# Second expert layer: second product by Strassen's scheme over pairs of weight blocks for two thirds of the tokens, with every prepared weight part kept in DRAM

## The chip, the cores and the metric

The kernel runs on one core of a Trainium2 chip. The metric is device time in microseconds (us): the median of three runs of the kernel before is 2180.21 us (2179.23 to 2182.91).

## What is computed

Three stages follow one another; all data are float32.

```python
# attention over pooled keys, 4 batches, 8 heads, 576 positions -> x [2304, 512]
x = (sigmoid(x @ w_gate) * (x @ w_val)) @ w_out        # first layer, inner width 1536
P = exp(x @ moe2_w_gate - max)                         # [2304, 8], then 8 rounds of row/column scaling
out = 0
for e in range(8):                                     # second layer, all 8 experts on all tokens
    h = maximum(x @ w1[e], 0.0)                        # w1[e]: 512 x 1024
    out += P[:, e:e+1] * (h @ w2[e])                   # w2[e]: 1024 x 512
```

Only the second layer changes. Every product is taken in three passes: each operand is split into a high part and a low part (value minus high), and high x high, high x low and low x high are summed.

## The kernel before

**Blocks and steps.** The 2304 tokens are 6 blocks of 384 (`TB`), taken as 3 pairs (`p`). For each pair the second layer walks 8 experts (`e`) and 4 quarters (`q`) of the inner width: 3 x 8 x 4 = 96 steps, the list `steps2` (L666). A step covers 256 inner columns (two halves of 128) for 768 tokens, and has two products.

**First product** (x with w1) goes by Strassen's scheme in Winograd's form: seven products P1 to P7 (L885) in place of eight, each 6 matmuls of 384 columns (`product`, L895). The sums of token blocks were stored earlier to DRAM (`xd`) and are loaded once per pair (`load_xf`, L722). The sums of w1 quarters are made in every step: `prep_w1` (L683) splits the raw weights into high parts (ScalarE) and low parts (GpSimd), tiles `fa` and `fs`. The results are combined in PSUM and in `c` tiles by VectorE, and `hidden` (L913) writes relu, high part (ScalarE) and low part (VectorE).

**Second product** (h with w2) is plain: `y_chunk` (L922) takes one chunk of 128 tokens: 6 matmuls of 512 columns into one PSUM bank `big`, and VectorE adds the bank, times the gate, to a running sum `acc`. A step has 6 chunks, which belong to the step before, so that they stand between P1 to P7 and give the other engines time. The weights are split in every step by `prep_w2` (L711).

**What sets the order.** The program is recorded in a hand-written order (`manual_schedule`); each engine runs its own instructions in that order and waits on semaphores. After each product a slot (`slot2`) issues one piece of weight preparation. All DMAs of this part are issued from SP's queue, in program order. `bank(tag, n)` hands out PSUM banks in rotation: 4 `big`, 2 `at`, 2 `gv`.

The weights of an expert's quarter are loaded and split three times, once per pair of token blocks.

Of the kernel before, what the change touches and what calls it, by code (L numbers as in the profile page):

```python
# [20 lines left out]
def attention_moe_moe_kernel(  # L21
# [647 lines left out]
    def load_w1(n):
        if n < len(steps2):  # L670
            _, e, q = steps2[n]
            raw1[n] = pools["late"].tile([128, 4, 2, 128], F32, tag="raw1", name="raw1", bufs=2)
            nc.sync.dma_start(out=raw1[n].rearrange("p a k f -> p (a k f)"), in_=moe2_w1[e, q])

    def load_w2(n):
        if n < len(steps2):
            _, e, q = steps2[n]
            raw2[n] = pools["more"].tile([128, 2, DM], F32, tag="raw2", name="raw2", bufs=2)
            nc.sync.dma_start(
                out=raw2[n], in_=moe2_w2[e].rearrange("(h g p) d -> g p h d", h=2, p=128)[q]  # L680
            )

    def prep_w1(n):  # L683


        if n >= len(steps2):
            return
        raw = raw1.pop(n)
        pool = pools["more" if n % 2 else "late"]
# [31 lines left out]

    def load_xf(p, i):  # L722
        if p < NPAIR:
            xf[p, i] = pools["late"].tile([128, 2, 2, TB], F32R, tag=f"xf{i}", name=f"xf{i}", bufs=1)
            nc.sync.dma_start(out=f32(xf[p, i]).rearrange("p s k c -> p (s k c)"), in_=xd[p][i])

    with tc.manual_schedule():
# [167 lines left out]
        def product(n, name, pt, start):  # L895

            (which, i), x = PRODUCTS[name]
            w = wsum[n][which]
            t = xf[steps2[n][0], x]
            m = 0  # L900
            for k in range(2):
                for s, o in PASSES:
                    nc.tensor.matmul(  # L903
                        out=pt[:, :TB],
                        lhsT=w[:, s, i, k],
                        rhs=t[:, o, k],
                        start=(start and m == 0),
                        stop=(m == 5),
                        skip_group_check=True,
                    )  # L910
                    m += 1
# [145 lines left out]
        for t in (3, 4, 5, 0, 1, 2):  # L1057
            y_chunk(len(steps2) - 1, t)
# [59 lines left out]
```

## Time and profile before

| | |
|---|---|
| median of 3 runs | 2180.21 us |
| span of the profiled execution | 2185.2 us |
| attention and first layer (to about 662 us) | the profile's first third |
| second layer, first pair of blocks (32 steps) | 684 to 1171 us, after a start-up from 662 us |
| second and third pair (64 steps) | 1170.9 to 2171.6 us |
| last chunks after the last step | 2171.6 to the end |
| TensorE busy over the span | 96% |

The profile shows one execution. "PE" is TensorE's matmuls, "PEld" its weight loads (one before each matmul), DVE is VectorE, ACT is ScalarE, POOL is GpSimd, SPq is SP's DMA queue. The time between the starts of two neighbouring matmuls is what a matmul costs in a stream; its own record is longer, since matmuls are pipelined.

### The profile page before, as it was taken

Reading aid. Unit: us, or ns where it says so; the run is one execution under the profiler, and the core shown is the slowest. Engines: PE = TensorE matmul, PEld = TensorE weight load, DVE = VectorE, ACT = ScalarE, POOL = GpSimd, SP = SyncE. Lnnn points to the kernel's source line nnn. Section 1 sums busy time; section 2 is a strip of 40 time slices with the busy share of each in tenths; the row PEclk is TensorE's granted clock in tenths of the full one; section 3 lists DMA queues with packets and bytes.
Section 4 is the critical chain, followed back from the end, with each engine's and each line's share of the span. In section 5 each row is a group of like instructions: output and inputs, shape, how many; then the busy total and the mean of one; then the engine's idle time right before and its main releaser. Section 6 shows DMA issues by size and latency. Waiting matters only on the chain.

```text
span 2185.2 us, 28656 instructions
## 1 busy us (share of the span) xinstructions
PE 2096.2 (96%) x10973; PEld 1905.0 (87%) x10973; DVE 1422.6 (65%) x2172; ACT 882.5 (40%) x1607; POOL 891.5 (41%) x780
## 2 busy tenths in 40 slices
PE   4679999999999999999999999999999999999999
PEld 4568989988997888888888898989888888898988
DVE  6846876644435877666666666666666666666665
ACT  4334343454544444434343434343433343434342
POOL 1100000353554465454545454545454545454541
PEclk8679999999999999999999999999999999999999
DMA  7432553453562132121215121212125212121211
GB/s 227 143 119 85 167 171 116 131 181 106 194 228 92 59 116 78 61 75 60 76 59 206 58 78 58 78 58 78 58 78 188 77 58 78 58 78 58 78 58 39
DMA packets 87451, 222.09 MB, mean 102 GB/s; under 512 B 8849, under 2 KB 8849, under 8 KB 87313
## 3 DMA queue, kind: packets, MB, share of 16 engines
q1 hardware_dynamic: 82128, 210.81, 28.5%
q10 hardware_dynamic: 5184, 9.44, 1.2%
q8 instruction: 86, 1.41, 0.3%
q14 instruction: 53, 0.43, 0.1%
HBM read 189.55 MB, written 30.67 MB: 101 GB/s over the span
## 4 chain that ended last, share of the span: by engine, by line
PE 86%; DVE 6%; issue 3%; ACT 2%; DMA 1%; POOL 1%; SPq 0%; ACTq 0%; DVEq 0%; POOLq 0%
PE big L934 37%; PE at L903 18%; PE gv L903 14%; PE gv L268 10%; PE big L560 4%; DVE wa_lo L236 1%; PE at L351 1%; DMA narrow<-made 1%; PE at L437 1%; DVE made L166 1%; DVE made L165 1%; DVE g L821 1%; ACT wa_hi L231 1%; PE at L422 0%; DVE wide L175 0%
## 5 line engine op out<-in xcount | busy, mean ns | idle before, releaser
L934 PE MATMUL big<-w2hl,h 128*128 128x512 f32 x3456 | 893.8, 394 | 0.0
L934 PEld LDWEIGHTS big<-w2hl,h 128*128 128x128 f32 x3456 | 642.0, 188 | 102.2
L963 DVE SCALAR_TENSOR_TENSOR acc<-big,prob,acc 128x512 f32<-128x512 f32 x516 | 385.6, 748 | 264.8 <-PE big L934 258.7
L705 POOL TENSOR_TENSOR fa<-raw,fa 128x768 fp32r<-128x768 f32 x96 | 179.4, 1869 | 440.0 <-PE big L934 403.2
L268 PE MATMUL gv<-xs,wa_hi 128*128 128x384 f32 x1152 | 314.6, 355 | 20.9 <-ACT xs L447 8.1
L707 POOL TENSOR_TENSOR fs<-ss,fs 128x512 fp32r<-128x512 f32 x96 | 125.0, 1303 | 292.9 <-ACT fs L704 289.3
L268 PEld LDWEIGHTS gv<-xs,wa_hi 128*128 128x128 f32 x1152 | 217.1, 198 | 28.2 <-ACT xs L447 8.9
L917 ACT ACTIVATE h<-gv 128x384 fp32r<-128x384 f32 x192 | 94.3, 491 | 355.2 <-DVE gv L1045 196.4
L903 PE MATMUL at<-xf,fa 128*128 128x384 f32 x1152 | 233.7, 338 | 0.8 <-DVE c L1038 0.8
L903 PE MATMUL at<-xf,fs 128*128 128x384 f32 x1152 | 232.4, 337 | 0.4 <-ACT c L1011 0.4
L903 PE MATMUL gv<-xf,fs 128*128 128x384 f32 x1152 | 231.6, 336 | 0.0
L717 DVE TENSOR_TENSOR w2hl<-raw,w2hl 128x512 fp32r<-128x512 f32 x192 | 227.6, 1186 | 6.1 <-ACT w2hl L716 6.1
L903 PEld LDWEIGHTS at<-xf,fa 128*128 128x128 f32 x1152 | 206.6, 189 | 17.7 <-DVE c L1038 1.6
L903 PEld LDWEIGHTS gv<-xf,fs 128*128 128x128 f32 x1152 | 205.4, 188 | 16.3
L268 PE MATMUL gv<-xs,wa_lo 128*128 128x384 f32 x576 | 203.1, 353 | 14.8 <-DVE wa_lo L236 11.8
L903 PEld LDWEIGHTS at<-xf,fs 128*128 128x128 f32 x1152 | 204.4, 188 | 9.0 <-ACT c L1011 0.7
L918 DVE SCALAR_TENSOR_TENSOR h<-gv,h 128x384 fp32r<-128x384 f32 x192 | 107.2, 558 | 107.6 <-ACT h L917 107.6
L560 PE MATMUL big<-h,wa_hi 128*128 128x384 f32 x576 | 150.8, 343 | 0.0
L594 POOL TENSOR_TENSOR fx<-x,fx 128x768 fp32r<-128x768 f32 x10 | 18.4, 1844 | 316.5 <-DVE x L577 263.4
L236 POOL TENSOR_TENSOR wa_lo<-stage,wa_hi 128x512 fp32r<-128x512 f32 x67 | 99.6, 1499 | 81.3 <-ACT wa_hi L231 69.6
L268 PEld LDWEIGHTS gv<-xs,wa_lo 128*128 128x128 f32 x576 | 114.7, 199 | 17.7 <-DVE wa_lo L236 14.6
L708 POOL TENSOR_TENSOR fs<-ss,fs 128x512 fp32r<-128x512 f32 x96 | 125.5, 1307 | 0.0
(149 smaller groups left out, 2682.1 us busy)
## 6 DMA issues: line engine op xcount, KB each, us to landing
raw<-in_moe_w_dram SPq DMA_DIRECT2D x192, 512.0 KB, 3.8
stage<-narrow SPq DMA_DIRECT2D x150, 256.0 KB, 2.8
xd<-fx SPq DMA_DIRECT2D x21, 768.0 KB, 3.3
xf<-xd SPq DMA_DIRECT2D x21, 768.0 KB, 6.6
narrow<-made ACTq DMA_DIRECT2D x36, 256.0 KB, 2.0
wide<-in_moe_w_gate_dram SPq DMA_DIRECT2D x12, 512.0 KB, 3.8
wide<-in_moe_w_val_dram SPq DMA_DIRECT2D x12, 512.0 KB, 10.0
wide<-in_moe_w_out_dram SPq DMA_DIRECT2D x12, 512.0 KB
```

What stands on the lines that cost most here:

```text
L236: eng.tensor_tensor(out=lo, in0=raw, in1=f32(hi), op=ALU.subtract)
L268: nc.tensor.matmul(out=out_, lhsT=a[s], rhs=b[m], start=(i == 0), stop=(i == n - 1))
L560: nc.tensor.matmul(out=x2p[d][:, :TB], lhsT=w[s][:, d * 128 : (d + 1) * 128], rhs=gs[j, f][m], start=(first and i == 0), stop=(last and i ...
L705: pl(out=fa[:, 1], in0=raw[:, 0:3], in1=f32(fa[:, 0]), op=ALU.subtract)
L707: pl(out=fs[:, 1, 0:2], in0=ss[:, 0:2], in1=f32(fs[:, 0, 0:2]), op=ALU.subtract)
L708: pl(out=fs[:, 1, 2:4], in0=ss[:, 2:4], in1=f32(fs[:, 0, 2:4]), op=ALU.subtract)
L717: nc.vector.tensor_sub(out=t[:, 1, i], in0=raw[:, i], in1=f32(t[:, 0, i]))
L903: nc.tensor.matmul(out=pt[:, :TB], lhsT=w[:, s, i, k], rhs=t[:, o, k], start=(start and m == 0), stop=(m == 5), skip_group_check=True,)
L917: nc.scalar.activation(out=t[:, 0], in_=src, func=AF.Relu)
L918: nc.vector.scalar_tensor_tensor(out=t[:, 1], in0=src, scalar=0.0, in1=f32(t[:, 0]), op0=ALU.max, op1=ALU.subtract)
L934: nc.tensor.matmul(out=py, lhsT=h[:, s, cs], rhs=w2hl[n][:, o, fh], start=(m == 0), stop=(m == 5))
L963: nc.vector.scalar_tensor_tensor(out=acc[t], in0=py, scalar=pr, in1=acc[t], op0=ALU.mult, op1=ALU.add)
```

## The change

For the first pair of blocks the steps stay as they are, but every prepared weight part is also stored to DRAM when it is made: `fa` and `fs` of each step (`fad`, `fsd`: 768 KB and 1 MB) and the split w2 (`w2d`: 1 MB). In the second and third pair (steps 32 to 95, `n >= NOLD`) `prep_w1` only loads `fa` and `fs` back, and `prep_w2` is not called.

In these two pairs the second product goes by Strassen's scheme too, over two steps at a time: the 2 x 2 parts of h are token blocks and inner halves, those of w2 are inner halves and output halves of 256 columns, and the two steps are summed in each product. It has seven products; each is taken for 3 chunks of 128 tokens, so 21 units (`UNITS`), and a unit is 6 matmuls of 256 columns (two steps x three passes). The units of two steps stand in the next two steps, as many per slot as `PER_SLOT` says: none in the first and last of the 14 slots. The right-hand operands are seven pieces of 512 KB per two steps: three quarters of w2, read back from `w2d`, and four sums (`t1`, `nt2`, `t3`, `nt4`). In the second pair of blocks the sums are made by GpSimd from the raw w2, split by ScalarE and GpSimd, and stored (`tsd`); in the third they are loaded. `PREP` gives the slot of each piece. The left-hand operands are h quarters and four sums of them (`h_sum`: sum on VectorE, high part on ScalarE, low part on GpSimd). `add_to` adds a bank or half a bank to the running sum.

At step 32 the last six chunks of the old kind run in one go, the pools `more` and `xring` are closed, and the pool `third` takes their place.

```diff
+    fsd = [dram.tile([128, 2048], F32, name=f"fsd{i}") for i in range(NOLD)]
+    fad = [dram.tile([128, 1536], F32, name=f"fad{i}") for i in range(NOLD)]
+    w2d = [dram.tile([128, 2048], F32, name=f"w2d{i}") for i in range(NOLD)]
+    tsd = [dram.tile([128, 4096], F32, name=f"tsd{i}") for i in range(NOLD // 2)]
...
+        if n >= NOLD:
+            fa = pool.tile([128, 2, 3, 2, 128], F32R, tag="fa", name="fa", bufs=1)
+            fs = pool.tile([128, 2, 4, 2, 128], F32R, tag="fs", name="fs", bufs=1)
+            wsum[n] = fa, fs
+            nc.sync.dma_start(out=f32(fa).rearrange("p s a k f -> p (s a k f)"), in_=fad[n % NOLD])
+            nc.sync.dma_start(out=f32(fs).rearrange("p s a k f -> p (s a k f)"), in_=fsd[n % NOLD])
+            return
...
+    PREP = {
+        3: (("t1", "sum"),),
+        4: (("b11", "load"),),
+        5: (("t1", "load"), ("nt2", "sum")),
+        6: (("nt2", "load"), ("t3", "sum")),
+        7: (("t1", "store"),),
+        8: (("t3", "load"), ("nt4", "sum"), ("nt2", "store")),
+        9: (("nt4", "load"),),
+        10: (("t3", "store"),),
+        11: (("b22", "load"), ("nt4", "store")),
+        13: (("b21", "load"),),
+    }
...
+        PER_SLOT = (0, 2, 2, 2, 3, 1, 1, 2, 2, 2, 2, 1, 1, 0)
...
+        def y_unit(n0, u):
+            h, w, col, i = UNITS[u]
+            if u < TPB:
+                banks[i] = bank("big", 4)
+            pt = banks[i]
+            o = pt[:, col * DH : (col + 1) * DH]
+            first = h in ("a11", "a12")
+            m = 0
+            for k in range(2):
+                for s, b in PASSES:
+                    nc.tensor.matmul(
+                        out=o,
+                        lhsT=hp[n0 + k, h][:, s, i * 128 : (i + 1) * 128],
+                        rhs=pieces2[n0, w][:, k, b],
+                        start=(first and m == 0),
+                        stop=(m == 5),
+                        skip_group_check=True,
+                    )
+                    m += 1
...
+        def y_slot(n, k):
+            k += 7 * (n % 2)
+            n0 = n - n % 2 - 2
+            if n0 >= NOLD:
+                u = sum(PER_SLOT[:k])
+                for i in range(PER_SLOT[k]):
+                    y_unit(n0, u + i)
+            for name, part in PREP.get(k, ()):
+                prep_piece(n - n % 2, name, part)
...
+            product(n, "P7", pa, False)
+            nc.vector.tensor_tensor(out=vc, in0=va, in1=c5, op=ALU.add)
+            low = h_direct(n, "a22", 3, vc)
+            s1, high = h_sum(n, "s1", 2, vc, a21, ALU.add)
+            high()
+            low()
+            settle(0)
+            done(4, 6)
...
+            if n >= NOLD:
+                if n == NOLD:
+                    for t in (3, 4, 5, 0, 1, 2):
+                        y_chunk(n - 1, t)
+                    third()
+                step(n)
+                continue
```

TensorE, a step of the third pair before (P1, P5, P6 and the chunks between; `h` tiles are left operands, `xf` token sums):

```order
L903 MATMUL at_17093<-xf0_14787,fa_16982 128x384 x6
L934 MATMUL big_17108<-w2hl_16987,h01_17035 128x512 x3
L934 MATMUL big_17108<-w2hl_16987,h11_17047 128x512 x3
L903 MATMUL gv_17094<-xf3_14814,fs_16983 128x384 x6
L934 MATMUL big_17133<-w2hl_16987,h01_17035 128x512 x3
L934 MATMUL big_17133<-w2hl_16987,h11_17047 128x512 x3
L903 MATMUL at_17093<-xf4_14836,fs_16983 128x384 x6
L934 MATMUL big_17153<-w2hl_16987,h01_17035 128x512 x3
L934 MATMUL big_17153<-w2hl_16987,h11_17047 128x512 x3
```

TensorE, the same stretch of the first step of two, changed:

```order
L1005 MATMUL at_11042<-xf0_10642,fa_10945 128x384 x6
L1005 MATMUL gv_11043<-xf3_10667,fs_10946 128x384 x6
L1157 MATMUL big_11065<-b11_10888,a11_10898 128x256 x3
L1157 MATMUL big_11065<-b11_10888,a11_11012 128x256 x3
L1157 MATMUL big_11074<-b11_10888,a11_10898 128x256 x3
L1157 MATMUL big_11074<-b11_10888,a11_11012 128x256 x3
L1005 MATMUL at_11042<-xf4_10687,fs_10946 128x384 x6
L1157 MATMUL big_11091<-b11_10888,a11_10898 128x256 x3
L1157 MATMUL big_11091<-b11_10888,a11_11012 128x256 x3
L1157 MATMUL big_11065<-t1_10911,s1_10884 128x256 x3
L1157 MATMUL big_11065<-t1_10911,s1_10997 128x256 x3
L1005 MATMUL gv_11043<-xf2_10708,fs_10946 128x384 x6
```

Chunks of 6 x 512 columns give way to units of 6 x 256; nothing stands between P1 and P5 of such a step any more.

SP's queue from step 32 on, changed (`rawp`: raw w2 of two steps; `b11`: a quarter of w2; `tsd0`: store of a sum):

```order
L1069 DMA out_0_dram<-acc_6507 128x512
L747 DMA rawp_10828<-in_moe2_w2_dram 128x2x512 x2
L699 DMA fa_10842<-fad1_167 128x1536
L700 DMA fs_10843<-fsd1_135 128x2048
L766 DMA b11_10888<-w2d0_198 128x2x256
L766 DMA b11_10888<-w2d1_199 128x2x256
L785 DMA tsd0_230<-t1_10911 128x1024
L699 DMA fa_10945<-fad2_168 128x1536
L700 DMA fs_10946<-fsd2_136 128x2048
```

Before, one step's part of this queue is two loads:

```order
L679 DMA raw2_13296<-in_moe2_w2_dram 128x2x512
L673 DMA raw1_13298<-in_moe2_w1_dram 128x1024
```

The queue carries more and larger transfers per step, and the load for step 34 (`fad2_168`) stands behind the store of a sum that GpSimd and ScalarE must have finished.

GpSimd in the first two steps of the second pair, changed (`ts`: raw sums of w2; `s1`, `n2`, `s3`, `s4`: low parts of the h sums in `hs`; `t1`, `nt2`: low parts of the w2 sums):

```order
L802 TENSOR_TENSOR ts_10871<-rawp_10828 128x512
L1096 TENSOR_TENSOR s1_10884<-hs_10882,s1_10884 128x384
L1096 TENSOR_TENSOR n2_10902<-hs_10900,n2_10902 128x384
L1096 TENSOR_TENSOR s3_10906<-hs_10904,s3_10906 128x384
L780 TENSOR_TENSOR t1_10911<-ts_10871,t1_10911 128x2x256
L802 TENSOR_TENSOR ts_10871<-ts_10871,rawp_10828 128x512
L1096 TENSOR_TENSOR s4_10925<-hs_10923,s4_10925 128x384
L780 TENSOR_TENSOR nt2_10929<-ts_10871,nt2_10929 128x2x256
L802 TENSOR_TENSOR ts_10871<-rawp_10828 128x512
```

The six w1 operations of a step are gone from GpSimd; the low parts of h sums and the w2 sums stand there instead.

## Rows read from the trace of the kernel before

**Rows 1.** The page: span, busy time and share of each engine, instruction counts.

```profile
span 2185.2 us, 28656 instructions
PE 2096.2 (96%) x10973; PEld 1905.0 (87%) x10973; DVE 1422.6 (65%) x2172; ACT 882.5 (40%) x1607; POOL 891.5 (41%) x780
```

**Rows 2.** The chain that ended last, share of the span by engine.

```profile
PE 86%; DVE 6%; issue 3%; ACT 2%; DMA 1%; POOL 1%; SPq 0%; ACTq 0%; DVEq 0%; POOLq 0%
```

**Rows 3.** Windows: length, busy time per engine (x count), granted clock, DMA share, GB/s.

```profile
1170.91:1671.30 500.39, 500.39 (x2495) 449.93 (x2494) 333.82 (x480) 198.19 (x352) 242.50 (x224) 1.00 0.23 82
1671.30:2171.60 500.30, 500.30 (x2494) 449.89 (x2493) 332.77 (x480) 195.98 (x349) 231.81 (x213) 1.00 0.21 71
```

**Rows 4.** Timeline of PE in one step: start us, us, engine, line, operation, operands, count.

```profile
1500.65 1.55 PE L934 MATMUL big<-w2hl,h 128*128 128x512 f32 x6
1502.04 1.21 PE L903 MATMUL gv<-xf,fs 128*128 128x384 f32 x6
1503.09 1.55 PE L934 MATMUL big<-w2hl,h 128*128 128x512 f32 x6
...
1516.31 0.87 PE L934 MATMUL big<-w2hl,h 128*128 128x512 f32 x3
```

**Rows 5.** Timeline of PE and PEld around two 8-column matmuls.

```profile
706.22 0.36 PEld L866 LDWEIGHTS big<-cs,ones 128*128 128x128 f32 x2
706.38 0.28 PE L866 MATMUL big<-cs,ones 128*128 128x8 f32 x2
706.49 0.48 PEld L903 LDWEIGHTS at<-xf,fs 128*128 128x128 f32 x3
```

**Rows 6.** Timeline of PE: 384-column matmuls behind 8-column weights.

```profile
671.67 0.51 PE L268 MATMUL big<-fx,wg_hi 128*8 128x384 f32 x2
672.01 0.34 PE L268 MATMUL big<-fx,wg_lo 128*8 128x384 f32 x1
```

**Rows 7.** Groups of instructions: busy us, mean ns of one, idle before.

```profile
L934 PE MATMUL big<-w2hl,h 128*128 128x512 f32 x3456 | 893.8, 394 | 0.0
L963 DVE SCALAR_TENSOR_TENSOR acc<-big,prob,acc 128x512 f32<-128x512 f32 x516 | 385.6, 748 | 264.8 <-PE big L934 258.7
L918 DVE SCALAR_TENSOR_TENSOR h<-gv,h 128x384 fp32r<-128x384 f32 x192 | 107.2, 558 | 107.6 <-ACT h L917 107.6
L917 ACT ACTIVATE h<-c 128x384 fp32r<-128x384 f32 x96 | 50.5, 526 | 107.5 <-DVE c L1038 107.5
L1011 ACT COPY c<-at 128x384 f32<-128x384 f32 x96 | 46.0, 480 | 178.4 <-PE at L903 178.4
L699 POOL TENSOR_TENSOR ss<-raw 128x256 f32<-128x256 f32 x96 | 72.9, 759 | 0.0
L707 POOL TENSOR_TENSOR fs<-ss,fs 128x512 fp32r<-128x512 f32 x96 | 125.0, 1303 | 292.9 <-ACT fs L704 289.3
```

**Rows 8.** Timeline of DVE and ACT after P3 and P7 of one step.

```profile
1508.84 0.49 ACT L917 ACTIVATE h<-gv 128x384 fp32r<-128x384 f32 x1 [1.61 <-DVE gv L1032]
1509.36 0.56 DVE L918 SCALAR_TENSOR_TENSOR h<-gv,h 128x384 fp32r<-128x384 f32 x1 [0.56 <-ACT h L917]
1509.83 0.55 DVE L1038 TENSOR_TENSOR c<-at,c 128x384 f32<-128x384 f32 x1
```

**Rows 9.** Windows at the switch to the second pair, columns as in rows 3.

```profile
1165.00:1170.00 5.00, 5.00 (x26) 4.47 (x25) 3.85 (x7) 1.45 (x3) 3.52 (x5) 1.00 0.94 338
1170.00:1175.00 5.00, 5.00 (x26) 4.43 (x26) 3.01 (x5) 2.37 (x6) 1.65 (x1) 1.00 1.01 396
```

**Rows 10.** Timeline of SP's queue at the same switch.

```profile
1156.33 13.55 SPq L725 DMA_DIRECT2D xf<-xd  x7
1174.16 13.54 SPq L967 DMA_DIRECT2D out_dram<-acc  x6
```

**Rows 11.** DMA issues: KB each, us from issue to landing.

```profile
raw<-in_moe_w_dram SPq DMA_DIRECT2D x192, 512.0 KB, 3.8
```

**Rows 12.** Timeline of PE at the end: the last chunks.

```profile
2171.60 9.72 PE L934 MATMUL big<-w2hl,h 128*128 128x512 f32 x42
```

More of the change, by code (lines that the diff above doesn't have):

```diff
@@ L718, in prep_w2, with load_pair @@
             yield
+        nc.sync.dma_start(out=w2d[n], in_=f32(t).rearrange("p s h d -> p (s h d)"))
+        yield
+    DH = DM // 2
+    pieces2 = {}
+    rawp = {}
+    def load_pair(n0):
+        if n0 < 2 * NOLD:
+            rawp[n0] = pools["more"].tile([128, 2, 2, DM], F32, tag="rawp", name="rawp", bufs=1)
+            for i in range(2):
+                _, e, q = steps2[n0 + i]
+                nc.sync.dma_start(
+                    out=rawp[n0][:, i], in_=moe2_w2[e].rearrange("(h g p) d -> g p h d", h=2, p=128)[q]
+                )
@@ new lines, in attention_moe_moe_kernel, with prep_piece @@
+    tsum = {}
+    QUARTER = {"b11": (0, 0), "b21": (1, 0), "b22": (1, 1)}
+    SUMS = ("t1", "nt2", "t3", "nt4")
+    def prep_piece(n0, name, part):
+        if n0 >= len(steps2):
+            return
+        k = n0 % NOLD
+        if part == "load":
+            w = pools["more"].tile([128, 2, 2, DH], F32R, tag=name, name=name, bufs=1)
+            pieces2[n0, name] = w
+            if name in QUARTER:
+                fh, d = QUARTER[name]
+                for i in range(2):
+                    nc.sync.dma_start(
+                        out=f32(w[:, i]),
+                        in_=w2d[k + i].rearrange("p (s h d) -> p s h d", s=2, h=2)[
+                            :, :, fh, d * DH : (d + 1) * DH
+                        ],
+                    )
+            elif n0 >= 2 * NOLD:
+                nc.sync.dma_start(
+                    out=f32(w).rearrange("p i s d -> p (i s d)"),
+                    in_=tsd[k // 2][:, SUMS.index(name) * 1024 : (SUMS.index(name) + 1) * 1024],
+                )
+            else:
+                src = tsum[n0][:, SUMS.index(name) % 2]
+                nc.scalar.activation(out=w[:, :, 0], in_=src, func=AF.Copy)
+                nc.gpsimd.tensor_tensor(out=w[:, :, 1], in0=src, in1=f32(w[:, :, 0]), op=ALU.subtract)
+            return
+        if n0 >= 2 * NOLD:
+            return
+        if part == "store":
+            nc.sync.dma_start(
+                out=tsd[k // 2][:, SUMS.index(name) * 1024 : (SUMS.index(name) + 1) * 1024],
+                in_=f32(pieces2[n0, name]).rearrange("p i s d -> p (i s d)"),
+            )
+            return
+        raw = rawp[n0]
+        b11, b12 = raw[:, :, 0, 0:DH], raw[:, :, 0, DH:DM]
+        b21, b22 = raw[:, :, 1, 0:DH], raw[:, :, 1, DH:DM]
+        if name == "t1":
+            tsum[n0] = pools["late"].tile([128, 2, 2, DH], F32, tag="ss", name="ts", bufs=1)
+        t = tsum[n0]
+        out, in0, in1, op = {
+            "t1": (t[:, 0], b12, b11, ALU.subtract),
+            "nt2": (t[:, 1], t[:, 0], b22, ALU.subtract),
+            "t3": (t[:, 0], b22, b12, ALU.subtract),
+            "nt4": (t[:, 1], t[:, 1], b21, ALU.add),
+        }[name]
+        nc.gpsimd.tensor_tensor(out=out, in0=in0, in1=in1, op=op)
+        if name == "nt4":
+            del rawp[n0]
+            load_pair(n0 + 2)
@@ new lines, in attention_moe_moe_kernel, with add_to @@
+        UNITS = [
+            (h, w, col, i)
+            for h, w, col in (
+                ("a11", "b11", 0),
+                ("s1", "t1", 1),
+                ("n2", "nt2", 0),
+                ("s3", "t3", 0),
+                ("a22", "nt4", 0),
+                ("s4", "b22", 1),
+                ("a12", "b21", 0),
+            )
+            for i in range(TPB)
+        ]
+        PER_SLOT = (0, 2, 2, 2, 3, 1, 1, 2, 2, 2, 2, 1, 1, 0)
+        banks = {}
+        def add_to(n0, half, i, src, cols, done=False):
+            p, e, q = steps2[n0]
+            t = half * TPB + i
+            tt = p * CPP + t
+            pr = prob[:, tt, e : e + 1]
+            if (p, t) not in acc2:
+                acc2[p, t] = pools["more"].tile([128, DM], F32, tag="acc", name="acc", bufs=6), set()
+            a, seen = acc2[p, t]
+            todo = [d for d in cols if d not in seen]
+            if todo and len(todo) < len(cols):
+                for d in cols:
+                    add_to(n0, half, i, src[:, (d - cols[0]) * DH : (d - cols[0] + 1) * DH], (d,))
+            else:
+                o = a[:, cols[0] * DH : (cols[-1] + 1) * DH]
+                if todo:
+                    nc.vector.tensor_scalar_mul(out=o, in0=src, scalar1=pr)
+                    seen.update(cols)
+                else:
+                    nc.vector.scalar_tensor_tensor(out=o, in0=src, scalar=pr, in1=o, op0=ALU.mult, op1=ALU.add)
+            if done and (e, q) == (E - 1, QF - 2):
+                nc.sync.dma_start(out=out[tt * 128 : (tt + 1) * 128], in_=a)
+                del acc2[p, t]
@@ new lines, in y_slot, with step, done @@
+        def y_slot(n, k):
[7 more added lines that the diff above has]
+                prep_piece(n - n % 2, name, part)
+        def step(n):
+            p, e, q = steps2[n]
+            last_of_pair = (e, q) == (E - 1, QF - 1)
+            pa = bank("at", 2)
+            pc = bank("gv", 2)
+            pb = bank("gv", 2)
+            load_w1(n + 2)
+            prep = prep_w1(n + 1)
+            def done(k, x=None):
+                if x is not None and last_of_pair:
+                    load_xf(p + 1, x)
+                if n >= NOLD:
+                    y_slot(n, k)
+                next(prep, None)
+            va, vb, vc = (t[:, :TB] for t in (pa, pb, pc))
+            product(n, "P1", pa, True)
+            c1 = c_tile()
+            nc.scalar.copy(out=c1, in_=va)
+            done(0, 0)
+            product(n, "P5", pc, True)
+            c5 = c_tile()
+            nc.scalar.copy(out=c5, in_=vc)
+            done(1, 3)
+            product(n, "P6", pa, False)
+            c2 = c_tile()
+            nc.scalar.copy(out=c2, in_=va)
+            done(2, 4)
+            product(n, "P3", pc, False)
+            nc.vector.tensor_tensor(out=vc, in0=vc, in1=c2, op=ALU.add)
+            a21 = pools["more"].tile([128, TB], F32, tag="a21", name="a21", bufs=2)
+            nc.scalar.activation(out=a21, in_=vc, func=AF.Relu)
+            done(3, 2)
+            product(n, "P7", pa, False)
[6 more added lines that the diff above has]
+            done(4, 6)
+            product(n, "P2", pb, True)
+            nc.vector.tensor_tensor(out=vb, in0=vb, in1=c1, op=ALU.add)
+            low = h_direct(n, "a11", 2, vb)
+            n2, high = h_sum(n, "n2", 2, vb, s1, ALU.subtract)
+            high()
+            s3, high = h_sum(n, "s3", 3, vb, a21, ALU.subtract)
+            high()
+            low()
+            settle(0)
+            done(5, 1)
+            product(n, "P4", pa, False)
+            low = h_direct(n, "a12", 3, va)
+            s4, high = h_sum(n, "s4", 3, va, n2, ALU.add)
+            high()
+            low()
+            settle(0)
+            done(6, 5)
@@ L970, in attention_moe_moe_kernel, with third @@
+        def third():
+            more_pool.__exit__(None, None, None)
+            xring_pool.__exit__(None, None, None)
+            pools["more"] = ctx.enter_context(
+                tc.tile_pool(name="third", bufs=1, side="right", reuse_waits="tile")
+            )
+            c_bufs[0] = 4
+            load_pair(NOLD)
         LATE = 2
@@ L988, in attention_moe_moe_kernel @@
                 sk = sinkhorn()
+                next(first_w, None)
             load_w2(n + 1)
@@ L1056, in attention_moe_moe_kernel @@
             slot2()
[L1057 to L1058 removed]
+        for u in range(len(UNITS)):
+            y_unit(len(steps2) - 2, u)
 _INS = [
```

58 lines of the change are left out of this document (50 added, 8 removed).

## The prediction

> **What bounds the kernel now.** I read the page first, then the chain, the windows of the second layer, and the matmuls of one step. TensorE is busy 96% of the span [rows 1] and is 86% of the chain that ended last [rows 2]. [...]
>
> What does a matmul cost there? Chunk, product and next chunk start at 1500.65, 1502.04 and 1503.09 [rows 4]: 6 matmuls of 512 columns take 1.39 us, 0.232 each, and 6 of 384 take 1.05, 0.175 each. Per column that is 0.453 and 0.456 ns: the cost goes by the columns, with no visible constant. From 1500.65 to 1516.31, the same place one step on, is 15.66 us, which is 42 x 0.174 + 36 x 0.232.
>
> **Step 1, the matmuls.** Two old steps have 72 matmuls of 512 columns for the second product: 72 x 0.232 = 16.70 us. The changed kernel has 21 units x 6 = 126 matmuls of 256 columns: 7/8 of the columns, but 54 more matmuls and weight loads. No row shows 256 columns behind 128-column weights. Two readings bound it.
> By columns it is 256 x 0.453 = 0.116 us. From below stands the weight load: where two matmuls move only 8 columns, loads start at 706.22, 706.39 (0.36 less the 0.19 of one record) and 706.49, so the last two are 0.10 to 0.11 apart [rows 5]; a 256-column matmul can't be cheaper than that, 0.110. The load itself is hidden at 384 columns: the interval is (672.01 - 671.67)/2 = 0.17 behind 8-column weights and 0.175 behind 128-column ones [rows 6, 4]. From above, 0.175, if it were no cheaper than 384 columns. I take 0.116: the load of 0.110 fits under it, though barely. Then 126 x 0.116 = 14.62 us, 2.08 less for two steps, and 32 such couples: **-66.6 us**. The ends: 0.110 gives 13.86 and -91 us; 0.175 gives 22.05 and +171. Break-even is 16.70/126 = 0.1325.
> The last old chunks run without products between them in 9.72 us for 42 [rows 12], with a record of 0.39 for the last one [rows 7], that is (9.72 - 0.39)/41 = 0.228 each, so the tail gains nothing to speak of (units there 0.114 to 0.116).
>
> [...]
>
> **Step 2, what must keep up in the steady state.** Per couple of steps PE then needs 84 x 0.174 + 14.62 = 29.24 us.
> - DVE: 20 operations on 384 columns (10 a step where 7 were: four sums of h come, one low part goes to POOL) at 0.558 [rows 7], 6 adds of 512 at 0.748, and 9 of 256. The last have no row; between 0.37 (the line through 0.558 and 0.748) and 0.558, I take 0.45. Together 19.7 us, 67%. The w2 splits go.
> - ACT: per step 7 reads of PSUM at about 0.49, 4 copies of sums at 0.526 [rows 7, 8]: 11 us; in the second pair four w2 sums of 512 are rounded as well, 0.6 to 0.7 each by the 0.526 for 384: some 13.5.
> - POOL: 8 low parts of 384, between 0.759 for 256 and 1.303 for 512 [rows 7], say 1.03, and in the second pair 8 operations of 512 at 1.303: 18.7 us of 29.2.
> None is full, so the question is order. The tightest place is P6 of the first step of a couple, which adds onto P1's bank and must wait for the copy c1. Between the end of the last P7 and that P6, PE has P2, P4, P1, P5 (4 x 1.05) and 4 units (4 x 0.70): 7.0 us. In that time DVE has eight operations of 384, which start 0.47 apart when nothing waits (1509.36 to 1509.83) [rows 8], two adds of 512 (0.66 apart by the same overlap), and one wait for a relu of 0.5: 5.6 us to the last sum; then ACT rounds it (0.53) and copies c1 (0.48): 6.6. It fits with some 0.3 us to spare. In the second pair ACT is queued behind POOL too: the roundings of nt2, t3 and nt4 each wait for a sum on POOL, and the copies c1 and c2 and three relus are queued behind them. By the same walk that eats the 0.3 us; I take 0.25 us for each of 16 couples, **+4 us**, with bounds 0 and 1.5 (one POOL operation late): 0 to 24 us.
>
> **Step 3, DMA.** Counted in MB: a step of the first pair moves 1.05 as before and stores 2.88 more, 3.93 in 15.66 us, 251 GB/s. A couple of the second pair moves 3.67 (fa, fs), 1.57 (quarters), 1.05 (raw w2) and 2.10 (stores): 8.39 MB in 29.2 us, 287 GB/s; one of the third 7.34 MB, 251 GB/s. At the old switch of pairs the engines, full at 0.94 and 1.01, moved 338 and 396 GB/s [rows 9]; I take 367. So 68 to 78% of what they did, with loads issued a whole step ahead: **0** in the steady state. In the first pair the stores only stand behind loads in SP's queue; a weight load lands 3.8 us after issue [rows 11] and is issued a step ahead: 0. If the quarters, read in pieces of 1 KB, moved at half the rate (no row shows such pieces), 4.3 us of engine time per couple would come on top and it would still fit.
>
> **Step 4, the switches.** At the first, xf loads are issued from 1156.3 to 1169.9 and outputs after 1174 [rows 10]. Now 8.4 MB (seven xf, fa/fs for step 32, a store) go between, 23 us at 367 GB/s, then outputs (1.57 MB, 4 us), raw w2 (2.9) and fa (2.1) and fs (2.9) for step 33. So fa lands near 1190 and fs near 1192.5. PE has six chunks to 1179.1 and then a step 32 of seven bare products, 7.3 us: it wants fa at 1186.4. It waits some 3.5 us there, 1.4 for fs, and about 1 in step 34, whose loads are queued behind a store that POOL must release: **+6 us**, bounds 0 and 15. At the second switch 10.5 MB (seven xf, fa/fs, four stores, two quarters) stand ahead of fa for step 65, 28.6 us where two steps take 29.2; with its own 2.1 and the way to landing it is some 3 us late: **+3**, bounds 0 and 8.
>
> **Sum.** -66.6 + 4 + 6 + 3 = -53.6 us. The profiled execution has a span of 2185.2 [rows 1], 5.0 above the median of the timed runs, so the span goes to 2131.6 and the timed median to 2180.2 - 53.6 = 2126.6, **2127 us**.
>
> **Rivals.**
> - *POOL, ACT or DMA make PE wait in every couple.* For it: the 0.3 us to spare, POOL's rough spans, four times the DMA bytes. Against: no engine above 70%. At 0.8 us in each of 32 couples more than I take, -28 us: 2152. Chance 0.14.
> - [...] Chance 0.04.
> - *The weight load is not covered at 256 columns: slower.* The mechanism is the load in front of each matmul, whose record is 0.188 us; where load and stream add up instead of overlap, each of the 4032 new matmuls costs 0.116 + 0.110 = 0.226, +11.8 us per couple, +377 us: 2570 with the 13 us of waits; a part of it, 0.140, gives +30 and so 2223. It decides from 0.129 on (break-even less 13 us over 4032 matmuls). Against: at 384 and 512 the loads cost nothing [rows 4, 6]. Chance 0.05.
> [...]
> - *The change does less than it says*, the old chunks staying in part: the instruction order has none after the six at step 32. Chance 0.
>
> **Chances.** The forecast's own range (0.114 to 0.118 a matmul, waits 4 to 20 us) is 2110 to 2142 with 0.77; the rivals are as given. No more than 2 in 10 is left out from 2106 to 2155. A difference under 0.2% (4.4 us) can't be told from none: faster 0.92, same 0.02, slower 0.06, the last with 0.01 for stalls beyond the first rival.
>
> **What would show it.** Six 256-column matmuls in 0.70 us and a couple of steps in 29.2 to 29.6; PE idle before the first matmuls of steps 33, 34 and 65, released by DMA; ACT's copy c1 ending close before P6. Wrong if six matmuls take 0.80 or more, or if PE is idle in every couple.

## The result, and the profile after

| | before | changed |
|---|---|---|
| median, us | 2180.97 (2179.23 to 2182.91, 4 runs) | 2195.56 (2194.05 to 2199.57, 4 runs) |
| ratio | 1 | 1.0068, 95% interval 1.0054 to 1.0082 |
| span of the profiled execution | 2185.2 | 2191.9 |
| couple of steps, 2nd pair / 3rd pair | 31.32 / 31.32 | 32.05 / 30.61 |

The change makes the kernel slower by 14.6 us; the forecast was 53 us faster. The page of the changed kernel (engine, busy us, share, instructions; then groups as in [rows 7]):

```profile
span 2191.9 us, 33642 instructions
PE 2053.2 (94%) x12701; PEld 1949.4 (89%) x12701; DVE 1330.7 (61%) x2338; ACT 849.1 (39%) x1671; POOL 824.2 (38%) x716
...
PE 64%; DVE 14%; ACT 7%; POOL 5%; issue 5%; DMA 5%; SPq 0%; DVEq 0%; ACTq 0%; POOLq 0%
...
L1005 PE MATMUL at<-xf,fs 128*128 128x384 f32 x1152 | 238.1, 341 | 40.2 <-ACT c L1208 38.7
```

TensorE has 43 us less to do than in [rows 1], and its share falls from 96 to 94%. The chain that ended last, 86% PE in [rows 2], now runs through DVE, ACT and POOL for a quarter of the span. One group of products has 40 us of idle time in front of it, and ACT's copy c at L1208 ends nearly all of that: it is c1, the copy of P1's bank, and P6 waits for it because P6 adds onto that bank. The windows of the same kernel, columns as in [rows 3], two stretches inside the second and third pair:

```profile
1300.00:1600.00 300.00, 283.66 (x1973) 279.98 (x1972) 168.05 (x328) 115.30 (x242) 165.01 (x147) 1.00 0.73 262
1700.00:2100.00 400.00, 391.91 (x2748) 389.27 (x2747) 235.19 (x460) 134.33 (x287) 104.58 (x104) 1.00 0.72 249
```

Where [rows 3] had no idle time, 16.3 us in 300 and 8.1 in 400 are idle now. The DMA share is three times as high (0.73 and 0.72) and under the 0.94 and 1.01 of [rows 9]; outside TensorE (PE and PEld) no engine is above 60%. The timeline of PE in the second pair shows both things that went wrong:

```profile
1379.70 1.32 PE L1005 MATMUL at<-xf,fs 128*128 128x384 f32 x6 [0.82 <-ACT c L1208]
...
1394.00 1.34 PE L1005 MATMUL at<-xf,fs 128*128 128x384 f32 x6 [0.95 <-ACT c L1208]
...
1397.65 1.59 PE L1157 MATMUL big<-t,s 128*128 128x256 f32 x12
1399.08 1.21 PE L1005 MATMUL at<-xf,fs 128*128 128x384 f32 x6
...
1409.32 1.59 PE L1157 MATMUL big<-nt,a 128*128 128x256 f32 x12
1411.75 1.31 PE L1005 MATMUL at<-xf,fs 128*128 128x384 f32 x6 [0.83 <-ACT c L1208]
```

Twelve matmuls of 256 columns take 1399.08 - 1397.65 = 1.43 us, 0.119 each; over all of them the median interval is 0.120. And P6 waits in each step: after the twelve from 1409.32 it could start at 1410.75 and starts at 1411.75, 1.00 us late (the idle time is shown as 0.83, since a record reaches 0.16 past the start of the next). A couple is 1411.75 - 1379.70 = 32.05 us; 84 x 0.174 + 126 x 0.120 = 29.7 without waits. Added up by that measure over steps 34 to 63 and 66 to 95, P6 waits 0.78 us in 15 first steps of the third pair, and 1.13 in 15 first steps and 0.98 in 15 second steps of the second pair; with 0.1 us each that the next matmuls are late behind it, 48 us.

Why c1 is late shows in the third pair, where a second step ends and the next first step begins (VectorE, ScalarE, PE; s1, n2, s3 and s4 are the four sums of h, and "rounding" one is ScalarE's writing of its high part):

```profile
1830.70 0.57 DVE L1224 TENSOR_TENSOR gv<-at,c 128x384 f32<-128x384 f32 x1 [0.37 <-PE at L1005]
...
1831.30 0.49 ACT L1085 ACTIVATE a<-gv 128x384 fp32r<-128x384 f32 x1 [2.00 <-DVE gv L1224]
1831.90 0.56 DVE L1092 SCALAR_TENSOR_TENSOR hs<-gv,a 128x384 f32<-128x384 f32 x1 [0.64 <-ACT a L1085]
...
1833.50 0.55 DVE L1232 TENSOR_TENSOR gv<-gv,c 128x384 f32<-128x384 f32 x1
...
1834.68 0.56 DVE L1092 SCALAR_TENSOR_TENSOR hs<-gv,hs 128x384 f32<-128x384 f32 x1 [0.63 <-ACT a L1085]
...
1836.74 0.55 DVE L1092 SCALAR_TENSOR_TENSOR hs<-at,hs 128x384 f32<-128x384 f32 x1
...
1837.33 0.52 ACT L1099 ACTIVATE s<-hs 128x384 fp32r<-128x384 f32 x1 [0.68 <-DVE hs L1092]
...
1837.76 0.46 ACT L1208 COPY c<-at 128x384 f32<-128x384 f32 x1
...
1838.27 0.97 PE L1005 MATMUL at<-xf,fs 128*128 128x384 f32 x4 [0.62 <-ACT c L1208]
```

VectorE's sums of s1 and n2 each wait for ScalarE's relu of the same bank: 1830.70 to 1831.90 and 1833.50 to 1834.68, 1.20 and 1.18 us from start to start where two such operations stand 0.47 apart in [rows 8]. The sum s4 starts at 1836.74, ScalarE rounds it at 1837.33, and c1 stands behind that in ScalarE's queue, though P1's stream had ended near 1835.0. In the second pair there is more in that queue (ScalarE, and one row of VectorE):

```profile
1378.65 0.63 ACT L779 ACTIVATE nt<-ts 128x512 fp32r<-128x512 f32 x1 [2.10 <-POOL ts L802]
1379.18 0.46 ACT L1208 COPY c<-at 128x384 f32<-128x384 f32 x1
...
1385.39 0.63 ACT L779 ACTIVATE nt<-ts 128x512 fp32r<-128x512 f32 x1 [2.29 <-POOL ts L802]
1385.92 0.47 ACT L1221 ACTIVATE a<-gv 128x384 f32<-128x384 f32 x1
...
1386.43 0.57 DVE L1224 TENSOR_TENSOR gv<-at,c 128x384 f32<-128x384 f32 x1 [0.71 <-ACT a L1221]
```

In second steps c1 is queued behind the rounding of nt2, which waits 2.10 us for POOL's sum. Later in the same second step the relu a21, behind P3, is queued behind the rounding of nt4; VectorE waits 0.71 us for it and starts that much later on the chain that ends in c1 of the next first step. That goes with the longer wait of first steps here, 1.13 us as against 0.78 in the third pair. At the first switch (PE, steps 32 and 33):

```profile
1176.85 1.26 PE L1005 MATMUL at<-xf,fa 128*128 128x384 f32 x6
1182.33 2.15 PE L1005 MATMUL at<-xf,fa 128*128 128x384 f32 x6 [4.21 <-DMA fa<-fad]
1184.96 1.73 PE L1005 MATMUL gv<-xf,fs 128*128 128x384 f32 x6 [0.48 <-DMA fs<-fsd]
1188.23 1.32 PE L1005 MATMUL at<-xf,fs 128*128 128x384 f32 x6 [1.55 <-ACT c L1208]
```

Steps 32 and 33 take 11.7 and 14.4 us where bare products need 7.3 each: 11.5 us more. The couple of steps 64 and 65 at the second switch takes 3.8 us more than a couple without waits, 1.5 of them P1 of step 65 waiting for fa. The six matmuls of 1182.33 have a record of 2.15 us, as against 1.26 one row up, and the windows of that stretch show the clock:

```profile
1178.00:1182.00 4.00, 0.11 (x1) 0.00 (x0) 2.27 (x5) 2.03 (x5) 1.45 (x2) 1.00 0.98 371
1182.00:1184.00 2.00, 1.68 (x6) 1.64 (x6) 1.02 (x2) 1.38 (x3) 2.00 (x3) 0.63 0.95 367
1184.00:1186.00 2.00, 1.51 (x5) 1.07 (x4) 0.00 (x0) 0.01 (x1) 2.00 (x3) 0.52 0.29 100
1186.00:1190.00 4.00, 2.45 (x14) 2.13 (x14) 0.00 (x0) 1.38 (x3) 4.00 (x4) 1.00 0.82 272
```

PE idles for 4 us, and the granted clock then is 0.63 and 0.52 in two windows of 2 us, before it is 1.00 again. The slow records cost nothing here, since what stands behind them waited for something else: P5 at 1184.96 for fs, and P6 at 1188.23 for c1, which ScalarE took up behind another late rounding:

```profile
1187.18 0.63 ACT L779 ACTIVATE nt<-ts 128x512 fp32r<-128x512 f32 x1 [3.18 <-POOL ts L802]
```

One loss stands outside the steps. The last 126 matmuls of 256 columns run without products between them, and there PE waits for VectorE's low part of a11 of the last step:

```profile
2172.88 1.81 PE L1157 MATMUL big<-b,a 128*128 128x256 f32 x13 [1.08 <-DVE a L1086]
```

From 2170.62 to the start of the last matmul that tail takes 17.2 us where 125 intervals of 0.120 are 15.0: 2.2 us.

### The profile page after: what moved, and what is told of

The parts are those of the page before. It is cut to its first block, busy times and chain, and to the rows that moved or that the text cites. A ratio compares the mean times of both kernels' runs of the same rounds, so it can differ in the third digit from the quotient of the medians.

```text
span 2191.9 us, 33642 instructions
## 1 busy us (share of the span) xinstructions
PE 2053.2 (94%) x12701; PEld 1949.4 (89%) x12701; DVE 1330.7 (61%) x2338; ACT 849.1 (39%) x1671; POOL 824.2 (38%) x716
## 4 chain that ended last, share of the span: by engine, by line
PE 64%; DVE 14%; ACT 7%; POOL 5%; issue 5%; DMA 5%; SPq 0%; DVEq 0%; ACTq 0%; POOLq 0%
PE big L1157 13%; PE at L1005 13%; PE big L1036 12%; PE gv L269 10%; PE gv L1005 9%; PE big L561 4%; DVE hs L1092 3%; DVE acc L1139 2%; DMA fa<-fad 2%; POOL ts L802 2%; ACT a L1085 2%; DVE wa_lo L237 1%; POOL t L780 1%; PE at L352 1%; DVE gv L1224 1%
## 5 line engine op out<-in xcount | busy, mean ns | idle before, releaser
L1096 POOL TENSOR_TENSOR s<-hs,s 128x384 fp32r<-128x384 f32 x192 | 194.4, 1013 | 426.8 <-ACT s L1099 258.4
L1139 DVE SCALAR_TENSOR_TENSOR acc<-big,prob,acc 128x256 f32<-128x256 f32 (+1 forms) x462 | 256.8, 584 | 101.7 <-PE big L1157 101.7
L1036 PE MATMUL big<-w2hl,h 128*128 128x512 f32 x1152 | 296.9, 394 | 0.0
L1005 PE MATMUL at<-xf,fs 128*128 128x384 f32 x1152 | 238.1, 341 | 40.2 <-ACT c L1208 38.7
L1036 PEld LDWEIGHTS big<-w2hl,h 128*128 128x128 f32 x1152 | 213.8, 188 | 34.4
L1005 PEld LDWEIGHTS at<-xf,fa 128*128 128x128 f32 x1152 | 199.1, 189 | 14.6 <-DMA fa<-fad 6.0
L1157 PE MATMUL big<-b,a 128*128 128x256 f32 x1152 | 164.2, 283 | 1.5 <-DVE a L1086 1.3
L1157 PE MATMUL big<-t,s 128*128 128x256 f32 x1152 | 162.7, 282 | 0.2 <-DVE acc L1139 0.2
L1157 PEld LDWEIGHTS big<-b,a 128*128 128x128 f32 x1152 | 156.2, 190 | 2.1 <-DVE a L1086 1.7
L1157 PEld LDWEIGHTS big<-t,s 128*128 128x128 f32 x1152 | 155.5, 189 | 0.4 <-DVE acc L1139 0.4
L1065 DVE SCALAR_TENSOR_TENSOR acc<-big,prob,acc 128x512 f32<-128x512 f32 x144 | 107.5, 747 | 70.3 <-PE big L1036 68.3
L1099 ACT ACTIVATE s<-hs 128x384 fp32r<-128x384 f32 x192 | 100.5, 523 | 90.9 <-DVE hs L1092 90.9
```

Source lines behind the costliest of these rows:

```text
L1005: nc.tensor.matmul(out=pt[:, :TB], lhsT=w[:, s, i, k], rhs=t[:, o, k], start=(start and m == 0), stop=(m == 5), skip_group_check=True,)
L1036: nc.tensor.matmul(out=py, lhsT=h[:, s, cs], rhs=w2hl[n][:, o, fh], start=(m == 0), stop=(m == 5))
L1065: nc.vector.scalar_tensor_tensor(out=acc[t], in0=py, scalar=pr, in1=acc[t], op0=ALU.mult, op1=ALU.add)
L1096: nc.gpsimd.tensor_tensor(out=t[:, 1], in0=x, in1=f32(t[:, 0]), op=ALU.subtract)
L1099: nc.scalar.activation(out=t[:, 0], in_=x, func=AF.Copy)
L1139: nc.vector.scalar_tensor_tensor(out=o, in0=src, scalar=pr, in1=o, op0=ALU.mult, op1=ALU.add)
```

## The experiments

Three sizes were in dispute: the interval at 256 columns, the waits at P6, and the DMA traffic.

**One part alone: 256-column matmuls.** The kernel before, with each chunk as two halves; Strassen's scheme and the DMAs stay out.

```
-    out=py, lhsT=h[:, s, cs], rhs=w2hl[n][:, o, fh]
+  for c0, c1 in ((0, 256), (256, 512)):
+    out=py[:, c0:c1], lhsT=h[:, s, cs], rhs=w2hl[n][:, o, fh, c0:c1]
```

> The kernel before, each chunk of the second product as two halves of 256 columns (12 matmuls instead of 6, all else as it was), so that nothing but the length of the matmuls changes. Theory C (a 256-column matmul costs 0.120, as in the trace of the changed kernel): 3456 x (2 x 0.120 - 0.232) = +28 us, 2209, between 2203 and 2215. Rival U (by columns alone 0.116, and the 0.120 of the changed kernel comes from its own waits): 0, 2181, and intervals of 0.116.

Measured: 2203.05 us, ratio 1.0107 [1.0086, 1.0128]; median interval 0.120, mean 0.1194. From its timeline of PE:

```profile
1500.93 1.60 PE L936 MATMUL big<-w2hl,h 128*128 128x256 f32 x12
1502.36 1.22 PE L903 MATMUL at<-xf,fa 128*128 128x384 f32 x6
```

1.43 us for twelve again, with DMA at its old rate (101 GB/s over the span, 102 before). So the 0.120 belongs to the matmul and not to the traffic: 3456 x (2 x 0.1194 - 0.2317) = +25 us, against 22 timed.

**Is 0.120 a floor or a fixed extra?** The same kernel with chunks of 288 and 224 columns.

```
-  for c0, c1 in ((0, 256), (256, 512)):
+  for c0, c1 in ((0, 288), (288, 512)):
...
```

> The kernel before, each chunk of the second product as 288 and 224 columns instead of 512: what sets the 0.120 us of a 256-column matmul? Theory W (the weight load in front of each matmul is a floor near 0.120): 288 columns 0.130 as by columns (0.453 ns each), 224 columns 0.120. Rival K (a fixed cost of 0.004 per matmul that shows below 384): 288 columns 0.134, 224 columns 0.105. Other values for 224 alone would mean a limit of its own for short matmuls.

Measured: 2225.41 us, a single run, of which only the intervals are used here: 0.1314 at 288 columns, 0.1103 at 224. Its timeline:

```profile
1501.11 1.61 PE L936 MATMUL big<-w2hl,h 128*128 128x288 f32 x12
1502.56 1.22 PE L903 MATMUL at<-xf,fa 128*128 128x384 f32 x6
```

(A row names the first shape only: six of each, 6 x 0.1314 + 6 x 0.1103 = 1.45.) Both theories miss. At 288 the cost is nearly the columns' (288 x 0.453 = 0.1305); at 224 it is the 0.110 that [rows 5] showed between loads, where the columns would give 0.1015. Near the crossing, at 256, it lies above both (0.120, where the columns give 0.116 and the loads of [rows 5] start 0.110 apart).

**One part alone: the parts in DRAM.** The kernel before, with prepared parts stored at first use and loaded in later pairs; second product as before.

```
+  if n >= NOLD:
+    nc.sync.dma_start(out=f32(fa)..., in_=fad[n % NOLD])
+    nc.sync.dma_start(out=f32(fs)..., in_=fsd[n % NOLD])
+    return
...
+  nc.sync.dma_start(out=w2d[n], in_=f32(t)...)
```

> The kernel before, with the prepared weight parts of the first pair stored to DRAM and loaded back in the second and third pair (fa, fs and the split w2, 2.88 MB a step), and the second product plain as before: the DRAM part of the change alone. If DMA and its queue cost nothing in the steady state, as the prediction said, it is within 0.2% of the kernel before, 2177 to 2186. Rival D (the loads come late): PE idle before P1 or P5 in many steps, 64 x 0.5 us and more, above 2200.

Measured: 2184.08 us (10 runs), ratio 1.0021 [1.0007, 1.0035], +3.5 us or so. Steady steps stay at 15.66. The only new waits of PE are one at each switch: the first chunk in steps 33 and 65 waits for the loaded w2, not P1 for fa. At the first:

```profile
1182.37 1.62 PE L953 MATMUL big<-w2hl,h 128*128 128x512 f32 x6 [0.88 <-DMA w2hl<-w2d]
```

Those two steps take 16.8 and 17.1 us in place of 15.66, 2.6 us together. This traffic is not the cause. It is less than the changed kernel's, though (a DMA share of 0.47 from 1300 to 1600 where that has 0.73); what settles the rest is the version with the roundings moved, below, which keeps all of it.

**One wait moved: s4's rounding.** The changed kernel, with ScalarE rounding s4 behind the next step's c1.

```
-            high()
+            late_high.append(high)
...
             nc.scalar.copy(out=c1, in_=va)
+            flush_high()
...
```

> The changed kernel with one move: in steps 32 to 95 ScalarE's rounding of the last h sum (s4, after P4) stands behind the next step's copy c1 instead of ahead of it. Theory Q (queue): P6 waits for c1, and c1 is queued on ScalarE behind the rounding of s4, which waits for VectorE's chain at the end of a step; then the wait before P6 in the first step of a couple (in the third pair 16 times, 0.80 us and 0.11 behind it; in the second pair 15 times, 1.13 and 0.11) vanishes, the wait in the second step of a couple in the second pair (16 x 1.03) stays, since c1 stands there behind a rounding that waits for GpSimd: 14 + 18 = 32 us less than the changed kernel's 2195.6, 2163, between 2158 and 2175. Rival F (full): VectorE and ScalarE are simply late by their work, and the wait comes back before P3 or P7 or in the next P6: at most 10 us less, 2185 to 2196.

Measured: 2164.49 us, ratio 0.9929 [0.9909, 0.9949], as expected. The group of products that had 40.2 us of idle time in front of it in the changed kernel has 13.8:

```profile
L1005 PE MATMUL at<-xf,fs 128*128 128x384 f32 x1152 | 235.9, 340 | 13.8 <-ACT c L1214 13.4 <-ACT c L1312 0.4
```

The waits of first steps are gone; those of second steps in the second pair stay (15 x 0.98).

**More of the queue: the roundings of nt2 and nt4 one slot later too.** Those of t1 and t3 stay where they were.

```
-  6: (("nt2", "load"), ("t3", "sum")),
-  7: (("t1", "store"),),
+  6: (("t3", "sum"),),
+  7: (("nt2", "load"), ("t1", "store")),
...
-  9: (("nt4", "load"),),
-  10: (("t3", "store"),),
+  10: (("nt4", "load"), ("t3", "store")),
```

> As the run before, and in the second pair of blocks ScalarE's roundings of two w2 sums that wait for GpSimd move: that of nt2 from ahead of c1 in the couple's second step to behind it (slot 6 to 7), that of nt4 from ahead of the relu after P3 to behind it (slot 9 to 10). Theory Q: the 16 waits of 1.03 + 0.11 us before P6 of second steps go too, another 18 us: 2145, between 2140 and 2158, so some 36 us under the kernel before (2181). Rival F: no more than 5 us below the run before.

Measured: 2147.01 us (2140.81 to 2150.36), ratio 0.9838 [0.9812, 0.9864]: faster than both kernels. Its windows and its PE timeline:

```profile
1300.00:1600.00 300.00, 300.00 (x2124) 300.00 (x2124) 182.23 (x355) 125.72 (x262) 181.83 (x161) 1.00 0.79 285
1700.00:2100.00 400.00, 400.00 (x2828) 400.00 (x2827) 241.95 (x471) 139.42 (x296) 106.75 (x106) 1.00 0.71 248
```

```profile
1850.08 1.21 PE L1004 MATMUL at<-xf,fs 128*128 128x384 f32 x6
...
1879.78 1.21 PE L1004 MATMUL at<-xf,fs 128*128 128x384 f32 x6
```

PE has no idle time again, and a couple is 29.70 us in both pairs, what the matmuls need at 0.120. The DMA share is 0.79 and 0.71, about what it was where PE waited (0.73 and 0.72), so the traffic is not what made it wait. The sum agrees: -66.6 + 16 for the matmuls, 14.7 at the two switches (9.7 and 5.0) and 2.2 in the tail make -34, as timed.

Some of the 9.7 is clock, in step 33:

```profile
1190.68 2.26 PE L1004 MATMUL gv<-xf,fs 128*128 128x384 f32 x6 [1.16 <-DMA fs<-fsd]
1192.74 2.12 PE L1004 MATMUL at<-xf,fs 128*128 128x384 f32 x6
```

```profile
1192.00:1194.00 2.00, 2.00 (x7) 2.00 (x7) 0.00 (x0) 1.00 (x2) 1.92 (x2) 0.50 0.79 262
```

Here products follow one another without a wait while the granted clock is 0.50: three of them, from 1190.68 to 1196.27, take 5.59 us where three at 1.00 take 3.15.

**The relu waits, first way.** The changed kernel, with a unit's addition put between VectorE's add and the sum that waits, in second steps, which add units of the couple before.

```
             low = h_direct(n, "a22", 3, vc)
+            if n % 2:
+                done(4, 6)
             s1, high = h_sum(n, "s1", 2, vc, a21, ALU.add)
...
```

> The changed kernel with VectorE's order changed in the second step of each couple alone: the add of a finished unit (the 19th, then the 20th) stands between the product's add and the h sum, where VectorE waited for ScalarE's relu. ScalarE's order is the changed kernel's. Theory Q says that c1 is late because VectorE waits twice for a relu (0.57 to 0.64 us idle before the sums s1 and n2) ahead of the sum s4, where the prediction's walk had one such wait: then the adds fill both waits, s4 and c1 come 1.1 to 1.3 us earlier, and the waits before P6 of first steps vanish (third pair 16 x 0.9, second pair 15 x 1.2, less what the queue behind GpSimd keeps), those of second steps stay: 22 to 32 us less than the changed kernel, 2164 to 2174. Rival A (ScalarE's own queue is what is late, VectorE's waits don't matter): no change, 2190 to 2200.

Measured: 2176.49 us (10 runs), ratio 0.9989 [0.9975, 1.0003]: 19 us off, fewer than the 22 to 32 expected. The view of waits for 1700 to 2130 (us in total, times, longest), the changed kernel first, then this one:

```profile
DVE hs L1092 <- ACT a L1085: 35.5, 56, 0.6
```

```profile
DVE hs L1092 <- ACT a L1085: 17.8, 28, 0.6
```

The filled waits are gone, and P6 of first steps waits 0.23 us in place of 0.78 in the third pair, 0.51 in place of 1.13 in the second; second steps still wait 1.00. So the relu waits were a part of the chain, and ScalarE's queue holds the rest.

**The relu waits, second way.** The changed kernel, with each sum ahead of the relu of its bank in the code.

```
-            low = h_direct(n, "a22", 3, vc)
             s1, high = h_sum(n, "s1", 2, vc, a21, ALU.add)
+            low = h_direct(n, "a22", 3, vc)
...
```

> The changed kernel, with the sums of h (s1, n2, s3, s4) read from their PSUM bank before ScalarE's relu of the same bank; in the changed kernel the relu comes first, and VectorE's sums of s1 and n2 wait 0.63 us each for it. Theory S (two engines' reads of one bank are put in the order in which the code has them, whichever that is): the wait does not go, it moves. ScalarE's relus now wait for the sums, VectorE's low parts wait for the relus, 0.6 us each as before, and ahead of the copy c1 ScalarE has the relu of a12 behind the sum s4 as well, 0.43 us more. First steps of a couple then wait 1.2 us (third pair) and 1.5 us (second pair) at P6 where they waited 0.80 and 1.13, second steps of the second pair up to 0.4 more: 14 to 21 us slower than the changed kernel's 2195.6, 2203 to 2217. Rival T (the wait is only VectorE's, since its sum stands behind the relu): the two waits of 0.63 us go, c1 comes 1.2 us earlier in the first steps, and the first steps' waits of 12.7 + 17.0 us fall to 5 or less: 2164 to 2174.

Measured: 2217.06 us (2208.56 to 2218.51), ratio 1.0171 [1.0153, 1.0189], 21 us slower than the changed kernel: theory S, at the edge of its range. The trace is of the run of 2208.56, 14.5 us above the changed kernel's profiled run. Its timeline at the same place of a step, and one row of the second pair:

```profile
1842.56 0.55 DVE L1092 SCALAR_TENSOR_TENSOR hs<-at,hs 128x384 f32<-128x384 f32 x1
1843.14 0.49 ACT L1085 ACTIVATE a<-at 128x384 fp32r<-128x384 f32 x1 [1.33 <-DVE hs L1092]
1843.53 0.51 ACT L1099 ACTIVATE s<-hs 128x384 fp32r<-128x384 f32 x1
...
1843.94 0.47 ACT L1208 COPY c<-at 128x384 f32<-128x384 f32 x1
...
1844.47 1.31 PE L1005 MATMUL at<-xf,fs 128*128 128x384 f32 x6 [1.26 <-ACT c L1208]
```

```profile
1425.25 1.88 PE L1157 MATMUL big<-b,a 128*128 128x256 f32 x12
```

Now the relu waits for the sum, although both only read the bank; in the two orders built, the wait is on whichever of the two comes second in the code, and neither order drops it. The idle time at P6 is 1.26 us where it was 0.62, and a couple of the third pair 31.29 in place of 30.61. One part missed: second steps of the second pair wait less at P6 (0.43 for 0.83), not more. First steps there wait more (1.33 for 0.95), so that the two cancel; couples still grow by some 0.25 us, since matmuls of a unit are late in each couple as well: the twelve from 1425.25 have a record of 1.88 where 1.59 is usual.

**The loads at the first switch.** The version with the three roundings moved, with raw w2 loaded behind fa and fs of step 33.

```
             done(0, 0)
+            if n == NOLD:
+                load_pair(NOLD)
...
-            load_pair(NOLD)
...
```

> The run defer_all (2147.0) with one move at the switch: the raw w2 of the second pair's first couple (1 MB) is loaded behind fa and fs of step 33 instead of ahead of them. In defer_all PE waits 3.84 us for fa before P1 of step 33 and 1.47 for fs before P5. If those waits are the queue's, they shrink by about the 2.9 us that 1 MB takes, and what is lost by a later first sum of w2 is under 2: 2144, between 2140 and 2148. Rival: the waits are those of the outputs or of the freed memory, which the move leaves: 2147.

Measured: 2152.87 us, ratio 0.9876 [0.9853, 0.9899]: a miss, 6 us slower than without (4.5 in the traces, from step 31 to the last matmul). P1 of step 33 waits 1.5 us in place of 3.8, but w2's first sums come later on POOL, ScalarE's copies are queued behind their roundings, and P6 and P3 wait 3.7 and 3.0:

```profile
1190.03 2.29 PE L1004 MATMUL at<-xf,fs 128*128 128x384 f32 x6 [3.36 <-ACT c L1213]
1194.97 2.29 PE L1004 MATMUL gv<-xf,fs 128*128 128x384 f32 x6 [2.65 <-ACT c L1220]
```

The granted clock is 0.50 from 1186 to 1194, and these products have records of 2.29 us instead of 1.21. What made it slower are the waits: they were moved and grew, from 5.3 us in front of P1 and P5 to 9.7 in front of P1, P5, P6 and P3.

## Why the prediction was wrong, by its steps

The sum was -66.6 + 4 + 6 + 3 = -53.6. With what the runs showed it is -66.6 + 16.1 for the matmuls, 47.9 of waits at P6, 15.3 at the switches and 2.2 in the tail: +14.9, against 14.6 timed.

- **Step 1, the matmuls**: right in kind, mis-sized. 0.120 in place of 0.116, 4032 x 0.004 = +16 us. The gain in matmul time is 51 us, not 67. "The load of 0.110 fits under it, though barely" was the right worry: near the crossing the measured 0.120 lies above both. That "the tail gains nothing to speak of" left out 2.2 us of waits there.
- **Step 2, the waits**: the step that failed, at "it fits with some 0.3 us to spare" (7.0 less 6.6 is 0.4). The walk counted VectorE's operations rightly (eight of 384, two of 512), but priced one relu wait at 0.5; the timeline has two, 0.73 and 0.71 more than the 0.47 spacing, so +0.94. From 1830.70 to c1's end at 1838.22 is 7.52 us, that is 6.6 + 0.94. PE's 7.0 us was right (P7's end near 1830.42, P6 free at 1837.48), and 0.28 between P7's end and VectorE's start was not priced at all: 7.52 + 0.28 - 7.06 = 0.74 late, P6's 0.8. For the second pair "by the same walk that eats the 0.3 us" was a guess: the rounding of nt2 ahead of c1, which the prediction names, cost 0.98 in every second step, a place that I did not walk. In all 48 us in place of 4; the upper bound of 24 was too low as well.
- **Step 3, DMA**: right. 0 in the steady state; with the parts alone 3.5 us timed, and the only new waits in that trace are at the switches.
- **Step 4, the switches**: place right, mechanism right in part, 11.5 and 3.8 us in place of 6 and 3. P1 of step 33 waits 4.4 for fa where 3.5 was forecast, and P1 of step 65 1.5 where 3 was. Step 34 does not wait for its loads. Left out were the waits in step 33 for what ScalarE does late: 1.7 at P6 and 1.2 at P7 for copies, and 1.7 at P4 for VectorE behind a relu.
- **The rivals**: the one of waits in every couple (0.14) was what happened, at 1.6 us a couple, twice its price, and with it the sign named for being wrong, PE idle in every couple. The slower rival was not it: loads are covered (PE and PEld are both busy 300.00 of 300.00 us above), and 0.120 is under its 0.129. Slower came from the waits, to which I gave 0.01 beyond the first rival's 2152.

ScalarE's order is what decided: with three roundings moved, and their low parts with them, the kernel is 34 us faster than before instead of 15 slower. In the trace of the changed kernel c1 started 0.43 us behind the rounding of s4 (1837.76 after 1837.33) and was late by that rounding's wait; moving the rounding alone took the wait out of first steps, 31 us.

## What to carry to other kernels

When products get shorter, walk the chain that feeds them back through every queue, for each kind of step, with each operation's recorded waits, before calling 0.3 us spare; a copy that frees PE goes ahead of any rounding that waits for another engine (31 us here for the rounding of s4 alone). Price a shorter matmul by a measured interval near its own length: where the columns alone come close to the 0.110 between the loads of [rows 5], this case had more than they give (3% at 256 columns, 9% at 224).

## What the runs showed of the hardware

- Intervals behind 128-column weights: 0.232 (512 columns), 0.175 (384), 0.131 (288), 0.120 (256), 0.110 (224). Down to 288 they go by the columns, within 1%. The last equals the 0.10 to 0.11 between two loads in [rows 5]; that the load sets it is inferred, since no run changes the load alone.
- After the idle times at the first switch (4.2 us; 3.7; or 1.4, 1.3 and 3.4 in close succession) TensorE ran at a granted clock of 0.50 for some 3.4, 6.8 and 13.6 us, an estimate from the windows' means with 0.50 and 1.00 as the two values; with waits of 0.8 to 1.1 us in the couples the windows have 1.00. Where products followed one another at the lower clock, the wait cost more than its own length (2.4 us more with the three roundings moved); where the next product waited for something else anyway, it did not.
- VectorE's sum and ScalarE's relu that read the same PSUM bank ran one after the other in both orders that were built: the second started some 0.6 us after the first (1831.90 after 1831.30, 1843.14 after 1842.56).
